# First slots of a fused attention and feed-forward kernel: one copy moved ahead of the exponentials, the weight pieces spread one to a slot, and one layout kept for the first chunk alone

## The chip, the cores and the metric

The kernel runs on one core of a Trainium2 chip. Times are microseconds of the device for one execution. Before the change the median of three runs is 655.12 us, from 654.51 to 655.52. The trace and the page of the profile come from a further execution, which took 657.56 us.

## The reference

Attention over a band, followed by two matrix products with a leaky ReLU between them:

```python
# q, k, v: (4 batches, 8 heads, 768 positions, 64)
scores = q @ k.T / 8 + bias            # bias: -slope[head] * distance
keep   = (key < n_global) | ((0 <= rel) & (rel < n_local))     # 8 and 96
a      = softmax(where(keep, scores, -1e9));   o = a @ v
x      = o.transpose(0, 2, 1, 3).reshape(3072, 512)
h      = x @ w_in                      # 512 x 2048, weights given as float64
out    = maximum(0.01 * h, h) @ w_out  # 2048 x 512
```

## The kernel before

**Attention units.** The attention is cut into 48 units `u` of one block of 128 queries and 4 heads, two units to a block, six blocks to a batch. Each unit has 192 gathered keys (128 in the first block of a batch). Here unit u passes through these steps:

- `scores(u)` (L181), TensorE: 8 small products, query and key, into PSUM.
- `biased(u)` (L195), VectorE: four instructions that add the bias and take the maximum.
- `exps(u)` (L210), ScalarE: four exponentials with their sums.
- `sums(u)` (L230, L231) on VectorE, then `dg` (L245) on GpSimd: reciprocals of the sums, put on diagonals.
- `transposes(u)` (L274), TensorE: 24 small products that transpose the probabilities and scale them by `dg`. Units from 14 on go another way, through DMAs.
- `keep_pt(u)` (L289, L293), ScalarE: the copy `pt` of the transposed probabilities out of PSUM. There is one buffer.
- `attn_v(u)` (L314, L326), TensorE: probabilities by values; called AV(u) below.
- `high_x(u)` (L339) on ScalarE and `low_x(u)` (L343) on VectorE: the result as two float32r parts, `xh` and `xl`.

`event(t)` puts these in a pipeline: AV(t-2), scores(t), transposes(t-1), then the work of the other engines, with `keep_pt(t-1)` last. So the copy of unit t-1 stands on ScalarE behind the exponentials of unit t, and AV(t-1) on TensorE in the next event waits for that copy.

**The `tall` layout.** For units 2 to 11 `tall(u)` is true: two of the three groups of keys lie on all 128 partitions, and AV uses 8 products of 128x64 (L326, `lhs, rhs = v[:, n, f, :], pt[:, n, f]`). Where it is false, the same keys lie on halves of 64 partitions, and there are 16 products of 64x64. `layout` on the host arranges `v` accordingly.

**FFN slots.** `order` is a list of pairs of a chunk (384 tokens, three blocks) and one of 16 column tiles of `w_in`. Slot j runs `ffn1(j)` (12 products, L797 to L799), then `ffn2(j-1)` (9 products, L818 to L820). The result of ffn1 is copied out by ScalarE (`t`, L801), goes through VectorE (L802), and becomes `gh` (ScalarE, L807) and `gl` (VectorE, L808). Events 0 to 7 run in a lead before the first slot; events 8 to 13 run in slots 1 to 6, one each, ahead of ffn1 in their slot.

**Weight pieces.** The float64 weights come in 32 pieces: piece 2f is column tile f of `w_in`, piece 2f+1 belongs to `w_out`. `conversion(p)` starts the loads of later pieces and returns three steps: `scale` (ScalarE, L560), `shift` (VectorE, L563 and L565) and `low` (VectorE, L569). Two more come after: `high` (ScalarE, L573) and `rest` (VectorE, L576). `conv_at` says which pieces a slot converts: the first of them goes with the event, others follow ffn1's steps. Up to the change piece 7 is converted before slot 0, and pieces 8 to 14 in slots 0 to 6. A piece's raw buffer is one of four (`STAGES`), freed by `low`.

**Order.** While `pinned[0]` holds, as it does here, each engine runs its instructions in the order in which the code issues them. The waits between engines are put in by the framework.

## Time and profile before

| | |
|---|---|
| median of three runs | 655.12 us (654.51 to 655.52) |
| profiled execution | 657.56 us, its span 656.0 us |
| TensorE matmuls | 632.2 us busy, 96% of the span |
| VectorE, ScalarE, GpSimd | 374.4, 283.0, 21.9 us busy |
| TensorE's granted clock | 0.99 over the span |

The page gives the busy time of each engine and the chain of work that ended last. The windows give busy time and granted clock of a stretch. A row of the timeline has start, duration, engine, line, operation, `out<-in`, shapes and a count; brackets at its end tell the idle time before it and what ended that. A float32 matmul of the small kind stands in the trace as two records, so that 8 products read x16.

### The profile page before, as it was taken

Reading aid. Unit: us, or ns where it says so; the run is one execution under the profiler, and the core shown is the slowest. Engines: PE = TensorE matmul, PEld = TensorE weight load, DVE = VectorE, ACT = ScalarE, POOL = GpSimd, SP = SyncE. Lnnn points to the kernel's source line nnn. Section 1 sums busy time; section 2 is a strip of 40 time slices with the busy share of each in tenths; the row PEclk is TensorE's granted clock in tenths of the full one; section 3 lists DMA queues with packets and bytes.
Section 4 is the critical chain, followed back from the end, with each engine's and each line's share of the span. In section 5 each row is a group of like instructions: output and inputs, shape, how many; then the busy total and the mean of one; then the engine's idle time right before and its main releaser. Section 6 shows DMA issues by size and latency. Waiting matters only on the chain.

```text
span 656.0 us, 14356 instructions
## 1 busy us (share of the span) xinstructions
PE 632.2 (96%) x5644; PEld 558.4 (85%) x5644; DVE 374.4 (57%) x1121; ACT 283.0 (43%) x796; POOL 21.9 (3%) x48
## 2 busy tenths in 40 slices
PE   5679999999999999999999999999999999999996
PEld 4568898988888888988989889889889889999985
DVE  6987778897667454654644645635645546232222
ACT  6976664555444342452443432443433524232221
POOL 3202210000000000000000000000000000000000
PEclk9898999999999999999999999999999999999998
DMA  8984444432766433443444444335343432010001
GB/s 278 348 305 148 163 164 144 139 97 95 217 208 224 137 85 113 142 153 112 162 129 138 148 129 122 126 106 175 121 137 131 153 118 90 8 49 1 0 1 52
DMA packets 55162, 88.04 MB, mean 134 GB/s; under 512 B 9776, under 2 KB 30256, under 8 KB 55088
## 3 DMA queue, kind: packets, MB, share of 16 engines
q1 hardware_dynamic: 55088, 87.06, 40.6%
q8 instruction: 46, 0.75, 0.5%
q14 instruction: 28, 0.23, 0.1%
HBM read 67.90 MB, written 19.14 MB: 133 GB/s over the span
## 4 chain that ended last, share of the span: by engine, by line
PE 89%; DVE 6%; ACT 2%; issue 1%; POOL 1%; DMA 0%; ACTq 0%; POOLq 0%; DVEq 0%
PE ps_h L797 14%; PE ps_o L820 13%; PE ps_h L798 13%; PE ps_h L799 13%; PE ps_o L818 13%; PE ps_o L819 13%; PE ps_v L181 2%; PE ps_v L326 2%; PE ps_av L181 1%; PE ps_v L314 1%; DVE w L569 1%; PE ps_av L326 1%; DVE w L565 1%; PE ps_tr L274 1%; PE ps_av L314 1%
## 5 line engine op out<-in xcount | busy, mean ns | idle before, releaser
L797 PE MATMUL ps_h<-xh,wih 128*128 128x384 f32 x512 | 175.8, 343 | 0.1
L798 PE MATMUL ps_h<-xl,wih 128*128 128x384 f32 x512 | 172.5, 337 | 0.0
L799 PE MATMUL ps_h<-xh,wil 128*128 128x384 f32 x512 | 172.3, 337 | 0.0
L802 DVE SCALAR_TENSOR_TENSOR t<-t 128x384 f32<-128x384 f32 x128 | 73.1, 571 | 144.7 <-ACT t L801 142.7
L801 ACT COPY t<-ps_h 128x384 f32<-128x384 f32 x128 | 61.3, 479 | 214.5 <-PE ps_h L799 214.5
L820 PE MATMUL ps_o<-woh,gl 128*128 128x512 f32 x384 | 152.1, 396 | 0.1
L818 PE MATMUL ps_o<-woh,gh 128*128 128x512 f32 x384 | 151.2, 394 | 1.0 <-ACT part L468 0.7
L819 PE MATMUL ps_o<-wol,gh 128*128 128x512 f32 x384 | 151.3, 394 | 0.0
L797 PEld LDWEIGHTS ps_h<-xh,wih 128*128 128x128 f32 x512 | 96.3, 188 | 10.3 <-ACT xh L339 3.1
L808 DVE TENSOR_TENSOR gl<-t,gh 128x384 fp32r<-128x384 f32 x128 | 71.3, 557 | 55.5 <-ACT gh L807 55.5
L798 PEld LDWEIGHTS ps_h<-xl,wih 128*128 128x128 f32 x512 | 96.3, 188 | 4.2
L799 PEld LDWEIGHTS ps_h<-xh,wil 128*128 128x128 f32 x512 | 96.2, 188 | 0.0
L807 ACT CAST gh<-t 128x384 fp32r<-128x384 f32 x128 | 65.5, 512 | 59.5 <-DVE t L802 58.7
L820 PEld LDWEIGHTS ps_o<-woh,gl 128*128 128x128 f32 x384 | 72.3, 188 | 18.0 <-DVE gl L808 2.2
L210 ACT ACTIVATE pr<-pr,nmall 128x192 f32<-128x192 f32 (+1 forms) x192 | 83.5, 438 | 3.6 <-DVE nmall L195 3.0
L818 PEld LDWEIGHTS ps_o<-woh,gh 128*128 128x128 f32 x384 | 72.2, 188 | 13.0 <-ACT part L468 1.2
L819 PEld LDWEIGHTS ps_o<-wol,gh 128*128 128x128 f32 x384 | 72.2, 188 | 11.2
L195 DVE CUSTOM_DVE_ANT_0 pr<-ps_v,nbw 128x192 f32<-128x192 f32 x88 | 25.3, 354 | 26.4 <-ACT xh L339 26.4
L210 ACT ACTIVATION_READ_ACCUMULATOR pr<-pr,nmall 128x1 f32 x192 | 36.4, 190 | 0.0
L237 DVE TENSOR_SCALAR pr<-pr,rs 128x192 f32<-128x192 f32 (+1 forms) x136 | 33.8, 312 | 1.0
L240 DVE STREAM_TRANSPOSE pr<-pr 128x768 f32<-128x768 f32 (+1 forms) x34 | 32.1, 945 | 0.9
L339 ACT CAST xh<-ps_v 128x256 fp32r<-128x256 f32 x28 | 10.5, 373 | 37.9 <-PE ps_v L181 36.2
(94 smaller groups left out, 462.7 us busy)
## 6 DMA issues: line engine op xcount, KB each, us to landing
kr<-in_kp_dram SPq DMA_DIRECT2D x40, 384.0 KB, 4.4
vr<-in_vp_dram SPq DMA_DIRECT2D x40, 320.0 KB, 4.5
via<-pr SPq DMA_DIRECT2D x30, 384.0 KB, 2.5
pt<-via SPq DMA_DIRECT2D x120, 96.0 KB, 2.3
wst<-in_wi_dram SPq DMA_DIRECT2D x16, 512.0 KB, 4.5
wst<-in_wo_dram SPq DMA_DIRECT2D x16, 512.0 KB, 3.9
qs<-in_qp_dram SPq DMA_DIRECT2D x24, 256.0 KB, 3.2
out_dram<-part SPq DMA_DIRECT2D x21, 256.0 KB, 2.1
```

Of the source, the lines that this page charges most:

```text
L210: pin(nc.scalar.activation(out=p, in_=p, func=AF.Exp, scale=-1.0, bias=nm[:, 2 * a + j:2 * a + j + 1], accum_out=sm[:, 2 * a + j:2 * a + j ...
L237: pin(nc.vector.tensor_scalar(out=p, in0=p, scalar1=rs[:, n:n + 1], scalar2=1.0, op0=ALU.mult, op1=ALU.mult))
L797: tc.keep_in_program_order(nc.tensor.matmul(ps, lhsT=wih[:, k, fs], rhs=xh[:, k, :CT], start=(k == 0), stop=False))
L798: tc.keep_in_program_order(nc.tensor.matmul(ps, lhsT=wih[:, k, fs], rhs=xl[:, k, :CT], start=False, stop=False))
L799: tc.keep_in_program_order(nc.tensor.matmul(ps, lhsT=wil[:, k, fs], rhs=xh[:, k, :CT], start=False, stop=(k == NK - 1)))
L801: pin(copy(out=t, in_=ps))
L802: pin(nc.vector.scalar_tensor_tensor(out=t, in0=t, scalar=0.01, in1=t, op0=ALU.mult, op1=ALU.max))
L807: pin(copy(out=gh, in_=t))
L808: pin(nc.vector.tensor_tensor(out=gl, in0=t, in1=gh.bitcast(F32), op=ALU.subtract))
L818: tc.keep_in_program_order(nc.tensor.matmul(o, lhsT=gh[:, ts_], rhs=woh[:, f, :], start=first, stop=False))
L819: tc.keep_in_program_order(nc.tensor.matmul(o, lhsT=gh[:, ts_], rhs=wol[:, f, :], start=False, stop=False))
L820: tc.keep_in_program_order(nc.tensor.matmul(o, lhsT=gl[:, ts_], rhs=woh[:, f, :], start=False, stop=last))
```

## The change

Four edits. `tall` holds for units 2 to 5 alone (`LEAD` is 6), and `layout` follows it. In events from 8 on `keep_pt(t-1)` is issued before `exps(t)`. Piece 7 is converted in slot 0, not ahead of the slots, and pieces 8 to 14 follow: slot 3 takes two, 10 and 11. The loop that ran the last parts of piece 6 and the whole of piece 7 ahead of slot 0 is gone; the parts of piece 6 now run among the steps of ffn1 in slot 0.

```diff
     def tall(u):
-        return u < BY_DVE and where(u)[2] > 0
+        return u < LEAD and where(u)[2] > 0
...
             if t == LEAD + 1:
                 high_x(t - 2, ov)
+            if mid and t >= LEAD + 2:
+                keep_pt(t - 1)
             exps(t)
...
         low()
-        if mid:
-            keep_pt(t - 1)
         if old and t <= LEAD:
             high_x(t - 2, ov)
+        if mid and t < LEAD + 2:
+            keep_pt(t - 1)
...
-    conv_at = {n: [n + LEAD_CONV + 1] for n in range(half)}
+    conv_at = {0: [7], 1: [8], 2: [9], 3: [10, 11], 4: [12], 5: [13], 6: [14]}
...
-    for step in (*due, *conversion(LEAD_CONV)):
-        if step in due:
-            due.remove(step)
-        step()
     behind = []
...
-    pe = [s for s in range(BY_DVE // NU) if s % NB]
+    pe = [s for s in range(CHUNKS[0]) if s % NB]
     vp[pe, :, :, :4] = vt[pe]
```

The lines below show instructions in the order in which an engine runs them. ScalarE, slots 0 and 1, before; the names `w_697`, `w_733`, `w_764`, `w_825` are pieces 6, 7, 8 and 9:

```order
L573 CAST wih<-w_697 128x4x128
L560 ACTIVATE w_733<-wst 128x512
L801 COPY t<-ps_h 128x384
L573 CAST woh<-w_733 128x512
L807 CAST gh<-t 128x384
L560 ACTIVATE w_764<-wst 128x512
L339 CAST xh<-ps_av 128x2x128
L573 CAST wih<-w_764 128x4x128
L560 ACTIVATE w_825<-wst 128x512
L210 ACTIVATE pr,sm<-pr,nmall 128x192 x4
L289 COPY pt<-ps_tr 128x2x6x64
```

The same stretch after, where lines below the edits have moved by two (L799 is L801 before) and `w_755`, `w_824` are pieces 7 and 8:

```order
L799 COPY t<-ps_h 128x384
L571 CAST wih<-w_697 128x4x128
L805 CAST gh<-t 128x384
L558 ACTIVATE w_755<-wst 128x512
L339 CAST xh<-ps_av 128x2x128
L571 CAST woh<-w_755 128x512
L558 ACTIVATE w_824<-wst 128x512
L289 COPY pt<-ps_tr 128x2x6x64
L210 ACTIVATE pr,sm<-pr,nmall 128x192 x4
```

Between the copy of slot 0's result and the copy `pt` of unit 7 there are now two scalings of weights (pieces 7 and 8) and two casts (6 and 7) and no exponentials; before, the cast of piece 6 and the scaling of piece 7 stood ahead of `t`, and the casts of 7 and 8, the scalings of 8 and 9 and the four exponentials behind it.

VectorE at the end of slot 3 and the start of event 11 before, where `w_1045` is piece 11:

```order
L802 SCALAR_TENSOR_TENSOR t<-t 128x384
L576 TENSOR_TENSOR wol<-w_1045,woh 128x512
L808 TENSOR_TENSOR gl<-t,gh 128x384
L195 ISA pr,nmall<-ps_av,nbw 128x192
L195 ISA nmall 128x1
```

The same place after, where `w_1060` is piece 10 and `w_1109` piece 11:

```order
L574 TENSOR_TENSOR wil<-w_1060,wih 128x4x128
L806 TENSOR_TENSOR gl<-t,gh 128x384
L561 TENSOR_SCALAR w_1109<-w_1109 128x512
L563 SCALAR_TENSOR_TENSOR w_1109<-wst,w_1109 128x512
L567 SCALAR_TENSOR_TENSOR w_1109<-wst,w_1109 128x512
L195 ISA pr,nmall<-ps_av,nbw 128x192
```

Three instructions for piece 11 stand between `gl` of slot 3 and `biased` of event 11; before, `gl` was followed by `biased` there.

TensorE at the start of slot 1 before (AV, scores, transposes, the first product of ffn1):

```order
L314 MATMUL ps_av<-pt,vr 64x128 x4
L326 MATMUL ps_av<-pt,vr 64x64 x8
L181 MATMUL ps_av<-kr,qs 64x192 x8
L274 MATMUL ps_tr<-dg,pr 64x64 x24
L797 MATMUL ps_h<-xh,wih 128x384
```

And after:

```order
L314 MATMUL ps_av<-pt,vr 64x128 x4
L326 MATMUL ps_av<-pt,vr 64x64 x16
L181 MATMUL ps_av<-kr,qs 64x192 x8
L274 MATMUL ps_tr<-dg,pr 64x64 x24
L795 MATMUL ps_h<-xh,wih 128x384
```

The second row goes from x8 to x16, here and in slots 2 to 6; the sizes in these rows are those of the result, so that the 128 or 64 partitions of the operands do not show. TensorE's order is otherwise the same, and so is GpSimd's. On SyncE's queue the loads of weight pieces 11 to 13 come one event later among the loads of queries, keys and values, and that of piece 14 comes behind the values of unit 11.

## The prediction

> **What bounds the kernel now.** I read the page first, then the waits of TensorE from the lead's end on, then the stretches around the one long wait.

> ```profile
> span 656.0 us, 14356 instructions
> PE 632.2 (96%) x5644; PEld 558.4 (85%) x5644; DVE 374.4 (57%) x1121; ACT 283.0 (43%) x796; POOL 21.9 (3%) x48
> ...
> PE ps_av L314 <- ACT pt L289: 3.5, 1, 3.5
> PE ps_o L818 <- ACT part L468: 0.7, 1, 0.7
> ```

> TensorE is the bound: 632 of 656 us. The last two rows are all that the list of its waits shows from 36 us to the end. So a saving counts where TensorE works or waits, and the one wait of size is that of AV(7) in slot 2 for the copy `pt` of unit 7.

> The windows (length, busy times, granted clock, DMA) show slot 1, the wait, slot 2, slot 3 and the rest:

> ```profile
> 38.82:45.96 7.14, 7.14 (x110) 5.83 (x109) 6.10 (x12) 3.58 (x8) 0.64 (x1) 1.00 0.70 234
> 45.96:49.50 3.54, 0.00 (x0) 0.00 (x1) 3.47 (x15) 3.54 (x12) 0.08 (x1) 0.87 0.91 323
> 49.50:59.00 9.50, 9.50 (x110) 7.99 (x110) 7.17 (x21) 6.35 (x17) 1.68 (x2) 0.69 0.48 165
> 59.00:65.90 6.90, 6.90 (x111) 5.90 (x110) 4.68 (x17) 4.47 (x14) 2.42 (x5) 1.00 0.45 124
> 84.00:650.00 566.00, 564.91 (x4433) 503.17 (x4432) 307.36 (x879) 220.75 (x607) 0.88 (x1) 1.00 0.37 117
> ```

> The wait costs twice. TensorE is idle for 3.54 us, with ScalarE busy for all of it. Then slot 2 takes 9.50 us where slot 3, with the same work, takes 6.90: the clock granted after the idle time is 0.69 over the slot. That is 2.60 us more, 6.14 together. After 84 us TensorE is idle for 1.09 us of 566.

> **Part 1: the copy and the pieces.** ScalarE and VectorE ahead of that wait, with SyncE's loads out of the picture:

> ```profile
> 38.33 0.66 DVE L569 SCALAR_TENSOR_TENSOR w<-wst,w 128x512 int32<-128x512 int32 x1
> 38.55 0.34 PE L799 MATMUL ps_h<-xh,wil 128*128 128x384 f32 x1
> 40.14 0.46 ACT L801 COPY t<-ps_h 128x384 f32<-128x384 f32 x1
> 43.92 0.42 DVE L563 TENSOR_SCALAR w<-w 128x512 int32<-128x512 int32 x1
> 45.11 0.69 DVE L569 SCALAR_TENSOR_TENSOR w<-wst,w 128x512 int32<-128x512 int32 x1
> 45.83 0.62 ACT L573 CAST wih<-w 128x512 fp32r<-128x512 f32 x1 [1.76 <-DVE w L569]
> 46.36 0.66 ACT L560 ACTIVATE w<-wst 128x512 f32<-128x512 f32 x1
> 46.92 0.44 ACT L210 ACTIVATE pr<-pr,nmall 128x192 f32<-128x192 f32 x1
> 48.67 0.78 ACT L289 COPY pt<-ps_tr 128x768 f32<-128x768 f32 x1
> 49.35 0.47 ACT L801 COPY t<-ps_h 128x384 f32<-128x384 f32 x1
> 48.87 0.17 DVE L230 TENSOR_SCALAR rs<-sm 128x4 f32<-128x4 f32 x1
> 49.42 0.88 POOL L245 TENSOR_TENSOR dg<-eye,rs 128x256 f32<-128x256 f32 x1 [9.96 <-DVE rs L231]
> 57.04 0.48 ACT L801 COPY t<-ps_h 128x384 f32<-128x384 f32 x1 [0.79 <-PE ps_h L799]
> 58.14 0.52 ACT L807 CAST gh<-t 128x384 fp32r<-128x384 f32 x1
> ```

> The result of ffn1(0) is there at 38.55 + 0.34 = 38.89, but its copy starts at 40.14, behind piece 7. The cast of piece 8 waits 1.76 us for `low` on VectorE, and `pt` comes behind that, a scaling, and 1.75 us of exponentials (46.92 to 48.67). The same durations in the new order give:

> - `t` of slot 0 at 38.95; `gh` 1.10 behind it (57.04 to 58.14), at 40.05, ending 40.57. The leftover parts of piece 6 fit beside: its `low` ends at 38.99.
> - `scale` of piece 7 from 40.47 to 41.15; `shift` and `low` take 1.88 (43.92 to 45.80), to 43.1. Its cast starts then; `scale` of piece 8 is 0.53 later (45.83 to 46.36), `pt` of unit 7 another 0.56 later (46.36 to 46.92), at 44.2, ending 44.97.
> - The exponentials of unit 8 start 0.68 behind it (48.67 to 49.35), at 44.9. Their sums come 1.95 later (46.92 to 48.87), `dg` starts 0.55 after that and lasts 0.88: it ends at 48.25.

> TensorE without a wait reaches AV(7) at 45.96 less the saving of part 2, 45.65. So `pt` is 0.7 us early and the wait goes, with the low clock behind it: 6.14 us.

> What is late next are the transposes, now behind `pt` and the exponentials. AV(7) and scores(9) take 0.73 + 0.70 us (rows of part 2), so transposes(8) are up at 47.08, and `dg` lets them go at 48.30: a new wait of 1.2 us in slot 2. I bound it by 0 and 2.07 (lead, below) and take 1.2. From there on slots recover: from `pt` to the next `pt` the ring is 0.68 + 1.95 + 0.55 + 0.88 and some 0.95 of transposes, 5.0 us, against a slot of 6.6.

> Slot 3 takes two pieces. The same walk, with 5.16 us from L274 to the next AV (60.74 to 65.90, rows of part 2): AV(8) at 48.30 + 5.16 = 53.46, scores(10) done at 53.46 + 0.73 + 0.88 = 55.07, then on ScalarE `xh` (about 0.3), `scale` (0.56) and `pt` (0.68): exps(10) at 56.7, their sums at 58.6, `low` of piece 10 to about 59.6. Behind it on VectorE come the leaky ReLU of slot 3 (0.6), with `gh` on ScalarE to 60.7, and `gl` to 61.2. Then VectorE spends 1.88 us on piece 11 ahead of `biased` of event 11 and of ScalarE's cast, to 63.1; 0.53 + 0.56 later, at 64.2, `pt` of unit 10 starts, exps(11) 0.68 later at 64.9, and `dg` ends 1.95 + 0.55 + 0.88 later, at 68.3. TensorE, by slots of 6.6, is at AV(10) at 66.64 (its `pt` is in time); with the shorter scores of unit 12 transposes(11) are up 1.2 us later, at 67.85: a wait of 0.5, bounds 0 and 1.3; I take 0.6, since each step of the walk can only be late. In the other slots the walk has `dg` 0.9 us or more ahead.

> Does a TensorE wait of 1.2 us lower the clock? The lead has both answers:

> ```profile
> 17.35 1.21 PE L274 MATMUL ps_tr<-dg,pr 64*64 64x64 f32 x48 [2.07 <-POOL dg L245]
> 25.48 0.57 PE L274 MATMUL ps_tr<-dg,pr 64*64 64x64 f32 x23 [1.44 <-POOL dg L245]
> 16.00:20.00 4.00, 2.65 (x80) 2.40 (x80) 3.93 (x16) 3.34 (x12) 0.88 (x1) 0.73 1.02 397
> 24.00:28.00 4.00, 2.27 (x84) 1.85 (x84) 3.93 (x16) 3.85 (x13) 0.88 (x1) 1.00 0.94 326
> ```

> A gap of 2.07 us goes with a clock of 0.73, one of 1.44 leaves it at 1.00. I take no loss at 1.2. [...]

> The rest has one answer each. SyncE: a load in the queue of piece 11 now waits for `low` of piece 7 (43.1) with the values of unit 9 behind it, which AV(9) needs at 60.0; the scaling of piece 11 comes at 60.6. Every piece is still complete a slot or more before its product (8 in slot 1 for slot 4, 11 in slot 4 for slot 6). If a load were late, TensorE would wait for the 4.5 us of its landing at most:

> ```profile
> wst<-in_wi_dram SPq DMA_DIRECT2D x16, 512.0 KB, 4.5
> 64.48 0.88 POOL L245 TENSOR_TENSOR dg<-eye,rs 128x256 f32<-128x256 f32 x1 [1.01 <-DVE rs L231]
> ```

> GpSimd stands idle for 1.01 us ahead of that `dg` although it rescales a table there; exponentials that come later only widen this.

> **Part 2: AV on halves.** AV in both layouts at full clock, the tall one of slots 3 and 4 and the other of later units:

> ```profile
> 59.00 0.45 PE L314 MATMUL ps_av<-pt,vr 64*64 64x128 f32 x8
> 59.38 0.73 PE L326 MATMUL ps_av<-pt,vr 128*64 128x64 f32 x16
> 60.04 0.88 PE L181 MATMUL ps_av<-kr,qs 64*64 64x192 f32 x16
> 60.74 0.88 PE L274 MATMUL ps_tr<-dg,pr 64*64 64x64 f32 x48
> 65.90 0.45 PE L314 MATMUL ps_av<-pt,vr 64*64 64x128 f32 x8
> ...
> 181.23 0.45 PE L314 MATMUL ps_av<-pt,vr 64*64 64x128 f32 x8
> 181.50 0.64 PE L326 MATMUL ps_av<-pt,vr 64*64 64x64 f32 x32
> 181.96 0.83 PE L181 MATMUL ps_av<-kr,qs 64*64 64x192 f32 x16
> ```

> From the first product of AV to the scores it is 60.04 - 59.00 = 1.04 us with 8 tall products, and 181.96 - 181.23 = 0.73 with 16 on halves: twice the records, 0.31 us less. Both ends shrink (0.38 to 0.27 ahead of L326, 0.66 to 0.46 behind), as if going over to the 128*64 form and back cost time each. Six units, 6 to 11: 1.86 us less, all on TensorE's path. Bounds: 0 and 2.0.

> **The sum.** 6.14 + 1.86 = 8.0 us saved, 1.2 + 0.6 of new waits, 6.2 net. The profiled execution would go from 657.56 to 651.4 (span 649.8); it stands 2.44 above the median of the runs, so from that, 655.12 - 6.2 = 648.9.

> **Rivals.**
> - *No new waits* (0.13): `dg` comes in time in slots 2 and 5. For it speaks the ring of 5.0 us, against it the walk. 655.12 - 8.0 = 647.1.
> - *The clock falls at the new wait* (0.07): the wait of slot 2 reaches 2 us, or the gate acts earlier than in the lead, and slot 2 loses its 2.6 us again. 651.5.
> - *ScalarE and VectorE are 2 us later in slot 1* (0.05), through the second scaling or a weight load. AV(7) then waits 1.3, `dg` is 3.2 late in all, the clock falls: 8.0 - 3.2 - 0.6 - 2.6 = 1.6 saved, 653.5.
> - *The records on halves cost what the tall ones do* (0.03): 0.66 / 16 = 41 ns each, 16 more are 0.66 us per unit, 4.0 in place of -1.9. Longer AVs hide 1.6 of the new waits, leaving 1.9 saved: 653.2. Against it stands the row of 32 records in 0.46 us, 14 ns each. [...]
> - *Slower* (0.03): the order `pt`, exponentials, sums, `dg`, transposes becomes the bound of the slots, with gaps at L274 over 2.07 us that drop the clock. One costs 2.07 + 2.6 = 4.7, two cost 9.4 against 8.0 saved: 656.5. It decides once the ring takes 6.6 + 2.07 = 8.7 us in two slots, 3.7 more than its rows add up to.
> - *It doesn't do what it says* (0.02): AV(7) still waits for `pt`, as something else stands ahead of it on ScalarE; only part 2 is left, and with new waits not even that. 655.

> **How the numbers follow.** The forecast, both new waits about as sized, has 0.67, from 648.0 to 650.2. A measurement here can tell about 0.2%, 1.3 us. The range takes in no new waits below (647.0) and the fallen clock above (651.5). Faster: 0.67 + 0.13 + 0.07 + 0.05 + 0.03, less a margin for what I have not seen: 0.93. Slower 0.03, within 0.2% 0.04.

> **What would show it.** The row of AV's wait for `pt` is gone from TensorE's waits, and the clock is 1.00 from 36 us on. In its place stand L274 waits for `dg`, once about 1.2 us near 47 and once about 0.6 near 68. AV in slots 1 to 6 reads x32 in the 64*64 form, with 0.73 us from L314 to L181. Slots 3 and 4 take 6.6 us. The prediction is wrong if a clock under 1.00 shows after 36 us, if waits at L274 recur in each slot, or if slots 1 to 6 together give back less than 5 us while TensorE has no wait there (the time then went to the lead or after 84 us).

## The result, and the profile after

The median of four runs each went from 655.32 to 651.36 us (ratio 0.9933, 95% interval 0.9908 to 0.9958), 4.0 us less. On two further occasions, beside the kernel before on the same chip, the ratios were 0.9915 (0.9896 to 0.9935) and 0.9929 (0.9905 to 0.9952): 5.6 and 4.7 us. 648.9 was forecast, in a range from 647.0 to 651.5.

The page after, and TensorE's waits from 36 us on. Lines below the edits have moved: L816 was L818, L795 was L797, L799 was L801.

```profile
span 650.7 us, 14540 instructions
PE 628.9 (97%) x5740; PEld 556.5 (86%) x5740; DVE 375.4 (58%) x1121; ACT 282.8 (43%) x796; POOL 22.2 (3%) x48
...
PE ps_av L326 <- issue: 1.3, 1, 1.3
PE ps_tr L274 <- POOL dg L245: 0.9, 1, 0.9
PE ps_o L816 <- ACT part L471: 0.7, 1, 0.7
PE ps_o L816 <- ACT gh L805: 0.2, 1, 0.2
```

AV's wait of 3.5 us for `pt` is gone. In its place stand a gap of 1.3 us that the profile puts down to no other engine ("issue"), and a wait of 0.9 for `dg`.

TensorE, ScalarE, VectorE and GpSimd around those places, from the timeline (start, duration):

```profile
38.43 0.45 PE L314 MATMUL ps_av<-pt,vr 64*64 64x128 f32 x8
40.27 0.52 PE L326 MATMUL ps_av<-pt,vr 64*64 64x64 f32 x21 [1.28 <-issue]
43.77 0.79 ACT L289 COPY pt<-ps_tr 128x768 f32<-128x768 f32 x1
44.45 0.46 ACT L210 ACTIVATE pr<-pr,nmall 128x192 f32<-128x192 f32 x1
46.43 0.17 DVE L230 TENSOR_SCALAR rs<-sm 128x4 f32<-128x4 f32 x1 [0.67 <-ACT pr L210]
46.98 0.88 POOL L245 TENSOR_TENSOR dg<-eye,rs 128x256 f32<-128x256 f32 x1 [7.89 <-DVE rs L231]
...
46.48 0.45 PE L314 MATMUL ps_av<-pt,vr 64*64 64x128 f32 x8
46.74 0.64 PE L326 MATMUL ps_av<-pt,vr 64*64 64x64 f32 x32
47.21 0.83 PE L181 MATMUL ps_av<-kr,qs 64*64 64x192 f32 x16
47.92 0.93 PE L274 MATMUL ps_tr<-dg,pr 64*64 64x64 f32 x48
...
68.44 0.93 PE L274 MATMUL ps_tr<-dg,pr 64*64 64x64 f32 x48 [0.88 <-POOL dg L245]
73.64 0.45 PE L314 MATMUL ps_av<-pt,vr 64*64 64x128 f32 x8
```

This execution is 0.39 us ahead at AV(6) (38.43 against 38.82). The walk of the prediction, less 0.39, had `pt` of unit 7 at 43.8, exps(8) at 44.5, the end of `dg` at 47.86, transposes(8) at 47.91 and AV(11) at 73.2. The rows have 43.77, 44.45, 46.98 + 0.88 = 47.86, 47.92 and 73.64. TensorE itself came to AV(7) at 46.48, where the walk less 0.39 had 45.26: the gap of 1.28 us at AV(6) lies between, and it takes up the time in which transposes(8) would have waited. AV on halves takes 47.21 - 46.48 = 0.73 us, as forecast.

The windows of slots 1, 2 and 5:

```profile
38.43:46.48 8.05, 6.77 (x127) 5.95 (x126) 6.82 (x20) 6.26 (x17) 0.66 (x1) 1.00 0.93 332
46.48:53.13 6.65, 6.65 (x127) 5.68 (x126) 6.25 (x21) 4.99 (x15) 1.24 (x2) 1.00 0.68 240
66.21:73.64 7.43, 6.55 (x126) 5.59 (x125) 6.52 (x22) 5.69 (x20) 2.72 (x6) 1.00 0.61 196
```

The clock is 1.00 in slot 2, where it was 0.69, and the slot takes 6.65 us where it took 9.50. From AV(6) to the start of ffn1 in slot 7 it is 79.64 - 38.43 = 41.21 us; before, 85.94 - 38.82 = 47.12. That is 5.9 us less in this pair, with 6.2 forecast from that profile. The open question was why medians show 4.0 to 5.6.

### The profile page after: what moved, and what is told of

The parts are those of the page before. It is cut to its first block, busy times and chain, and to the rows that moved or that the text cites. A ratio compares the mean times of both kernels' runs of the same rounds, so it can differ in the third digit from the quotient of the medians.

```text
span 650.7 us, 14540 instructions
## 1 busy us (share of the span) xinstructions
PE 628.9 (97%) x5740; PEld 556.5 (86%) x5740; DVE 375.4 (58%) x1121; ACT 282.8 (43%) x796; POOL 22.2 (3%) x48
## 4 chain that ended last, share of the span: by engine, by line
PE 89%; DVE 4%; ACT 3%; DMA 1%; issue 1%; POOL 0%; SPq 0%; POOLq 0%; DVEq 0%; ACTq 0%
PE ps_h L795 14%; PE ps_h L797 13%; PE ps_h L796 13%; PE ps_o L818 13%; PE ps_o L817 13%; PE ps_o L816 13%; PE ps_v L181 3%; PE ps_v L326 2%; PE ps_v L314 1%; DMA kr<-in_kp_dram 1%; PE ps_av L181 1%; ACT pr L210 1%; DVE w L567 1%; PE ps_av L326 1%; DVE w L563 1%
## 5 line engine op out<-in xcount | busy, mean ns | idle before, releaser
L795 PE MATMUL ps_h<-xh,wih 128*128 128x384 f32 x512 | 175.6, 343 | 0.1
L797 PE MATMUL ps_h<-xh,wil 128*128 128x384 f32 x512 | 172.4, 337 | 0.0
L799 ACT COPY t<-ps_h 128x384 f32<-128x384 f32 x128 | 61.2, 478 | 214.8 <-PE ps_h L797 214.8
L816 PE MATMUL ps_o<-woh,gh 128*128 128x512 f32 x384 | 151.2, 394 | 1.0 <-ACT part L471 0.7
L818 PE MATMUL ps_o<-woh,gl 128*128 128x512 f32 x384 | 152.0, 396 | 0.1
L795 PEld LDWEIGHTS ps_h<-xh,wih 128*128 128x128 f32 x512 | 96.0, 188 | 10.4 <-ACT xh L339 3.1
L797 PEld LDWEIGHTS ps_h<-xh,wil 128*128 128x128 f32 x512 | 96.0, 188 | 0.0
L805 ACT CAST gh<-t 128x384 fp32r<-128x384 f32 x128 | 65.7, 513 | 59.4 <-DVE t L800 58.6
L818 PEld LDWEIGHTS ps_o<-woh,gl 128*128 128x128 f32 x384 | 72.3, 188 | 17.8 <-DVE gl L806 2.0
L210 ACT ACTIVATE pr<-pr,nmall 128x192 f32<-128x192 f32 (+1 forms) x192 | 83.7, 441 | 3.5 <-DVE nmall L195 3.0
L816 PEld LDWEIGHTS ps_o<-woh,gh 128*128 128x128 f32 x384 | 72.2, 188 | 13.1 <-ACT part L471 1.1
L210 ACT ACTIVATION_READ_ACCUMULATOR pr<-pr,nmall 128x1 f32 x192 | 36.8, 192 | 0.0
## 6 DMA issues: line engine op xcount, KB each, us to landing
wst<-in_wi_dram SPq DMA_DIRECT2D x16, 512.0 KB, 4.2
wst<-in_wo_dram SPq DMA_DIRECT2D x16, 512.0 KB, 4.0
```

Source lines behind the costliest of these rows:

```text
L210: pin(nc.scalar.activation(out=p, in_=p, func=AF.Exp, scale=-1.0, bias=nm[:, 2 * a + j:2 * a + j + 1], accum_out=sm[:, 2 * a + j:2 * a + j ...
L795: tc.keep_in_program_order(nc.tensor.matmul(ps, lhsT=wih[:, k, fs], rhs=xh[:, k, :CT], start=(k == 0), stop=False))
L797: tc.keep_in_program_order(nc.tensor.matmul(ps, lhsT=wil[:, k, fs], rhs=xh[:, k, :CT], start=False, stop=(k == NK - 1)))
L799: pin(copy(out=t, in_=ps))
L805: pin(copy(out=gh, in_=t))
L816: tc.keep_in_program_order(nc.tensor.matmul(o, lhsT=gh[:, ts_], rhs=woh[:, f, :], start=first, stop=False))
```

## The experiments

Two theories for the missing time. A: the low clock behind the wait was read from one long execution and is worth less in the median. B: the changed kernel gives time back, in the gap of 1.3 us and the wait of 0.9. Neither covers the spread of the rest. From the start of ffn1(7) to the end of the span the products are the same in every kernel here, yet that stretch took from 567.9 to 571.1 us in the fourteen profiles (570.1 in the prediction's, 571.1 in the first of the changed kernel), and the lead up to AV(6) took from 38.1 to 41.3.

The number compared below is therefore the distance from AV(6) to ffn1(7), which covers slots 1 to 6, from the timelines (differences of start times):

| kernel | us | slots 1 and 2 | slot 5 |
|---|---|---|---|
| before, two profiles | 47.12, 45.42 | 20.18, 18.42 | 6.75, 6.74 |
| changed, three profiles | 41.21, 41.21, 41.38 | 14.70, 14.71, 14.88 | 7.43, 7.42, 7.38 |
| order_only | 42.01 | 14.71 | 7.00 |
| halves_only | 41.88 | 16.48 | 6.32 |
| conv_only | 41.90 | 14.90 | 6.70 |
| keep_only | 46.78 | 19.79 | 6.74 |
| before_filled | 44.74 | 17.75 | 6.70 |
| late_pair | 41.14 | 14.71 | 6.35 |
| no_pair | 40.21 | 14.72 | 6.35 |
| slot0_free | 43.31 | 14.60 | 6.33 |
| copy_behind | 40.02 | 14.51 | 6.32 |

**before_again: the kernel before, unchanged.**

> The kernel before, unchanged, for what differs between its own executions. Theory A (the clock term was read from one long execution): the stretch from AV(7) to AV(8), 9.50 us in the execution that the prediction used, is shorter in most executions, since the low clock covers less of it; spans spread over 2 us or more, and the median lies about 2 us under that execution. Theory B (the changed kernel gives time back): slot 2 takes about 9.5 us here in each execution, spans lie within 1 us of each other, and the missing time must be looked for in the changed kernel (a gap of 1.3 us in slot 1, a wait of 0.9 us in slot 5).

656.7 against 656.27 us (ratio 1.0002, 0.9987 to 1.0017); single executions of the kernel before lie from 654.1 to 658.9 on that chip. Windows of its wait, slot 2 and slot 3:

```profile
48.31:51.26 2.95, 0.00 (x1) 0.01 (x1) 2.88 (x11) 2.95 (x11) 0.08 (x1) 1.00 0.86 309
51.26:59.70 8.44, 8.44 (x109) 7.34 (x109) 7.17 (x21) 6.34 (x17) 1.68 (x2) 0.80 0.54 185
59.70:66.66 6.96, 6.96 (x110) 5.94 (x110) 4.74 (x17) 4.53 (x14) 2.41 (x5) 1.00 0.47 164
```

Wait and low clock cost 2.95 + (8.44 - 6.96) = 4.4 us here, and 6.14 in the profile of the prediction. That is theory A's sign. The spread doesn't come from there alone, though: AV(6) starts at 41.28 here and at 38.82 there, and this execution was the longest of its twelve (658.38) with the cheaper wait.

**order_only: the order and the pieces, without the new layout.**

```diff
-        return u < LEAD and where(u)[2] > 0
+        return u < BY_DVE and where(u)[2] > 0
```

(beside the changed kernel; `layout` likewise)

> The copy ahead of the exponentials and the pieces one slot later, with the tall layout for units 2 to 11 as before. By the prediction's terms: 6.1 us less than before, less about 0.6 us of waiting for dg in slot 2 and none in slot 5 (tall AVs are longer, dg is in time): 5.5 us saved. Theory A: 2.5 to 4 us saved, as the clock term is worth less. Theory B: 4 to 5.5 us. In both the wait of AV(7) for pt is gone and the clock is 1.00 in slot 2.

Ratio 0.9924 (0.9902 to 0.9946), 5.0 us less. In its profile transposes(8) wait 0.69 us for `dg`, as sized (0.6):

```profile
48.84 0.93 PE L274 MATMUL ps_tr<-dg,pr 64*64 64x64 f32 x48 [0.69 <-POOL dg L245]
```

5.0 is above what I wrote for theory A and within B's figures. With the 0.69 added back, wait and clock together are worth some 5.7 us here, which speaks against theory A's smaller clock term, though the interval (3.5 to 6.4 saved) holds less too.

**halves_only: the layout alone, beside the kernel before.**

```diff
-        return u < BY_DVE and where(u)[2] > 0
+        return u < LEAD and where(u)[2] > 0
```

> Only the layout: units 6 to 11 on halves, order and pieces as before. The wait of AV(7) for pt stays and takes in what AV(6) saves; AV(7) to AV(11) save 0.31 us each and AV(7), at a low clock, up to 0.6: 1.3 to 1.9 us less than before by the prediction, in theory A and B alike. If the rows on halves cost more in these slots than in the later ones, no gain or a loss.

Ratio 0.9957 (0.9941 to 0.9973), 2.8 us less (1.8 to 3.9), more than the 1.3 to 1.9 expected. Its wait and slots 2 and 3 show why a single profile is a poor price for the clock:

```profile
46.72:50.04 3.32, 0.00 (x1) 0.00 (x1) 3.25 (x13) 3.32 (x12) 0.08 (x1) 1.00 0.91 322
50.04:56.59 6.55, 6.55 (x126) 5.79 (x126) 6.46 (x20) 5.86 (x16) 1.68 (x2) 1.00 0.60 201
56.59:63.13 6.54, 6.54 (x127) 5.78 (x126) 5.65 (x19) 4.98 (x15) 2.41 (x5) 1.00 0.61 212
```

TensorE is idle for 3.32 us and the clock stays at 1.00: the same kind of gap cost 2.60 us in one execution, 1.48 in another and nothing here. Five AVs at 0.31 are 1.55 us. Slots 3 and 4 shrink by more than that: 6.54 us each, where they took 6.90 and 6.91. The rest of the 2.8 may be the clock or the spread, and isn't settled.

**before_filled: needless products in the wait.**

```diff
             ov = av = ps_x.tile([P, 2, 512], F32, tag="ps_av", name="ps_av")
+            if t == LEAD + 3:
+                for _ in range(12):
+                    tc.keep_in_program_order(nc.tensor.matmul(av[:, 0, :CT], lhsT=wih[:, 0, :P], rhs=xt[0][0][:, 0, :CT],
+                                                              start=True, stop=True))
             attn_v(t - 2, ov)
```

> The kernel before with 12 needless products of 128x384 ahead of AV(7), in the PSUM columns that the scores of unit 9 overwrite: they work in the time in which TensorE waits for pt, 2.1 us of it, so that the idle gap is about 1.2 us and not 3.3. AV(7) starts when it did. Theory A (part of the old cost was the clock, and it varies): slot 2 runs at clock 1.00 in 6.9 us, and the median is lower by the clock term alone, 1 to 2 us. If the clock term is the 2.6 us of the first profile in each execution: 2.6 less. If the clock doesn't matter for the median: the same time.

Ratio 0.9977 (0.9962 to 0.9992), 1.5 us less, interval 0.5 to 2.5. Doing more work made the kernel faster:

```profile
47.86 2.32 PE L365 MATMUL ps_av<-xh,wih 128*128 128x384 f32 x12 [1.44 <-DVE xl L343]
50.11 0.45 PE L314 MATMUL ps_av<-pt,vr 64*64 64x128 f32 x8
50.11:57.01 6.90, 6.90 (x111) 5.90 (x110) 6.63 (x20) 5.81 (x17) 1.55 (x2) 1.00 0.56 196
```

AV(7) starts no earlier than in the kernel before (10.85 us after AV(6); 10.68 and 9.98 there), and slot 2 runs at full clock in 6.90 us. So by this run the clock term is worth about 1.5 us in the median, with 2.60 just outside the interval. This is theory A's number. Other runs leave room for more: with a wait of 3.2 us (3.54 and 2.95 in the two profiles of the kernel before), order_only's 5.7 leaves 2.5 for the clock.

**conv_only and keep_only: the two halves of the order, beside the kernel before.** conv_only takes the new `conv_at` and drops the loop ahead of slot 0; keep_only moves the copy:

```diff
+            if mid and t >= LEAD + 2:
+                keep_pt(t - 1)
             exps(t)
...
-        if mid:
-            keep_pt(t - 1)
+        if mid and t < LEAD + 2:
+            keep_pt(t - 1)
```

> The pieces one slot later, with the copy pt still behind the exponentials and the layout as before. By the walk pt of unit 7 comes 1.75 us later than with the copy ahead, at 46.0 to 46.7, so AV(7) waits about 0.8 us; dg of unit 8 is 0.7 earlier and transposes(8) do not wait. Nearly all of order_only's gain is here: 4 to 4.6 us less than before. Rival: the copy's move carries the gain, and this one saves less than 2 us.

> The copy ahead of the exponentials alone, pieces and layout as before. pt of unit 7 comes 1.75 us earlier, so AV(7) waits 1.7 us in place of 3.3, but the exponentials of unit 8 end 0.7 later than before while TensorE is ahead, and transposes(8) wait for dg about 1.5 us. The waits move: 0.2 us saved, and the clock term (0 to 2 us) if two shorter gaps leave the clock up. Rival: the copy carries the gain, 4 us saved.

conv_only: ratio 0.9937 (0.9915 to 0.9960), 4.1 us less, with a wait of AV(7) for `pt` of 0.98 us and none for `dg`. keep_only: 0.9985 (0.9971 to 0.9999), 1.0 us less. The pieces carry the gain. The row of conv_only, and those of keep_only:

```profile
47.52 0.45 PE L314 MATMUL ps_av<-pt,vr 64*64 64x128 f32 x8 [0.98 <-ACT pt L289]
...
48.39 0.45 PE L314 MATMUL ps_av<-pt,vr 64*64 64x128 f32 x8 [1.80 <-ACT pt L289]
51.69 1.56 PE L274 MATMUL ps_tr<-dg,pr 64*64 64x64 f32 x48 [1.27 <-POOL dg L245]
48.39:59.22 10.83, 9.56 (x110) 8.08 (x110) 8.93 (x26) 8.06 (x25) 1.76 (x2) 0.68 0.61 210
```

The copy halves the wait of AV(7) and puts what it gains into a wait for `dg`, as walked (1.7 and 1.5 expected). The clock is 0.68 over the slot. By the windows (0.76 from 48 to 52 us, 0.50 from 52 to 56) it fell at about 50.07 us, before the second gap began (50.42): behind a gap of 1.80 us here, where it stayed behind one of 3.32 in halves_only.

**late_pair, no_pair, slot0_free: where the second piece goes, beside the changed kernel.**

```diff
-    conv_at = {0: [7], 1: [8], 2: [9], 3: [10, 11], 4: [12], 5: [13], 6: [14]}
+    conv_at = {0: [7], 1: [8], 2: [9], 3: [10], 4: [11], 5: [12, 13], 6: [14]}     # late_pair
+    conv_at = {0: [7], 1: [8], 2: [9], 3: [10], 4: [11], 5: [12], 6: [13, 14]}     # no_pair
+    conv_at = {1: [7], 2: [8], 3: [9], 4: [10, 11], 5: [12, 13], 6: [14]}          # slot0_free
```

> The changed kernel with its pair of pieces in slot 5 (12 and 13) and not in slot 3, so that piece 11 no longer stands ahead of biased of event 11. The wait of transposes(11) for dg in slot 5, 0.88 us in the changed kernel's profile, goes; piece 13 now delays unit 13, whose transposes come only in slot 23. Prediction: 0.6 to 0.9 us less than the changed kernel, so about 4.7 us less than before where the changed kernel has 4.0. [...]

late_pair: ratio 0.9920 (0.9897 to 0.9944), among the changed kernel's three (0.9915 to 0.9933), and 41.14 us: the 0.6 to 0.9 us expected were not gained. The wait in slot 5 is gone (6.35 us), but it comes back in slot 7, where ffn1 needs the buffer that ScalarE empties too late, behind the exponentials that piece 13 delayed:

```profile
78.75 0.45 ACT L799 COPY t<-ps_h 128x384 f32<-128x384 f32 x1
79.25 0.44 PE L795 MATMUL ps_h<-xh,wih 128*128 128x384 f32 x1 [0.78 <-ACT t L799]
```

> The changed kernel with one piece in each of slots 0 to 5 (7 to 12) and the pair 13 and 14 in slot 6, whose second piece stands ahead of no event. The wait for dg in slot 5 goes (0.9 us) and, other than with the pair in slot 5, nothing stands between the result of slot 6 and its copy t, so it isn't given back: 0.9 us less than the changed kernel, AV(11) 34.3 us after AV(6), and ffn1(7) 0.9 us earlier against AV(6). Rival: another wait takes it (the copy t or gl in slot 7), and the stretch from AV(6) to ffn1(7) is 41.2 us as in the changed kernel.

no_pair: ratio 0.9905 (0.9883 to 0.9928) where the changed kernel beside it had 0.9929, and 40.21 us in place of 41.2 to 41.4: by the traces the 0.9 us expected are gained and kept; the intervals of the times overlap.

> The changed kernel with no piece in slot 0: 7, 8, 9 in slots 1 to 3, pairs in slots 4 and 5. dg of unit 8 is then ready more than 1 us before transposes(8). It tells what the gap of 1.2 us at AV(6) costs. If the gap only covers a wait for dg that would come anyway, and depends on the order of ScalarE, it goes and slots 1 and 2 are 1.2 us shorter. [...]

slot0_free: ratio 0.9944 (0.9923 to 0.9965), slower than the changed kernel by the traces (43.31 us against 41.38), while the intervals overlap. Slot 1 keeps its gap (1.28 us, 8 records into L326 as in the changed kernel) with another order on ScalarE, and no_pair, whose order up to slot 2 is the changed kernel's, has none: so ScalarE's order is not its cause. The pairs bring a wait of 0.85 for `dg` in slot 6 and one of 1.99 for `t` in slot 7, behind which the products of ffn1 follow each other at 0.32 us from 83.15 to 86.03, where they do so at 0.17 in no_pair's slot 2:

```profile
41.13 0.52 PE L326 MATMUL ps_av<-pt,vr 64*64 64x64 f32 x21 [1.28 <-issue]
75.49 0.69 PE L274 MATMUL ps_tr<-dg,pr 64*64 64x64 f32 x32 [0.85 <-POOL dg L245]
82.59 0.44 PE L795 MATMUL ps_h<-xh,wih 128*128 128x384 f32 x1 [1.99 <-ACT t L799]
```

What the gap costs in the changed kernel is told by no_pair, whose slot 1 has none and whose slot 2 then waits for `dg`:

```profile
45.74 0.45 PE L314 MATMUL ps_av<-pt,vr 64*64 64x128 f32 x8
48.69 0.93 PE L274 MATMUL ps_tr<-dg,pr 64*64 64x64 f32 x48 [1.39 <-POOL dg L245]
```

Slots 1 and 2 take 14.72 us there and 14.70 to 14.88 with the gap. The gap lies in time that TensorE would have spent waiting for `dg`: beside that wait, the gap costs 0.2 us at most. One or the other is paid in full: without both, slots 1 and 2 take 6.54 (no_pair) and 6.55 us (halves_only), 1.6 less.

**after_third and copy_behind: the changed kernel, and it with the copy behind the exponentials again.** after_third runs the changed kernel as it is; after_again, on another occasion, did so too.

```diff
-            if mid and t >= LEAD + 2:
-                keep_pt(t - 1)
             exps(t)
...
-        if mid and t < LEAD + 2:
+        if mid:
             keep_pt(t - 1)
```

> The changed kernel once more, beside many executions of the kernel before on one chip. Terms as measured so far (wait about 3.2 us, low clock behind it of 0 to 2.6 and in the median some 1.5, AVs 1.9, new waits 1.2 and 0.9): 4.0 to 5 us less than before, and slot 2 at clock 1.00 in its profile. By the prediction's own sum: 6.2 less. The gap of 1.3 us at AV(6) stands in its profile again, and no wait for dg in slot 2 beside it.

> The changed kernel beside the three variants below on one chip: 4.5 to 5.5 us less than before. In its profile AV(11) starts 35.2 us after AV(6), with a gap of about 1.2 us at AV(6) and a wait of 0.9 us for dg in slot 5, as in the two profiles of it so far.

Ratios 0.9915 and 0.9929, 5.6 and 4.7 us less, the first of them more than the 4.0 to 5.0 expected; both profiles show about the same distance, gap and wait as the first.

> The changed kernel with the copy pt behind the exponentials in each event, as before the change. By the rows pt of unit 7 comes 1.75 us later and AV(7) waits; the gap at AV(6) covers 1.2 us of it, so 0.3 to 0.6 us of wait are left in slot 2; dg of units 8 and 11 is 0.7 us earlier, so slot 5 waits 0.2 and not 0.9. About the time of the changed kernel, within 0.5 us: the copy's move is worth next to nothing beside the pieces. Rival: the copy carries the gain, and this kernel is 2 us or more slower than the changed one.

copy_behind: ratio 0.9894 (0.9874 to 0.9915), 648.64 us where the changed kernel beside it had 650.62. It has the lowest ratio of the study, which overlaps with no_pair's. The two were expected within 0.5 us of each other. Its only wait in slots 1 to 6:

```profile
47.15 0.45 PE L314 MATMUL ps_av<-pt,vr 64*64 64x128 f32 x8 [1.34 <-ACT pt L289]
```

No wait for `dg` comes in slot 5 (6.32 us). From AV(6) to ffn1(7) it is 40.02 us, 1.2 less than in the changed kernel: beside the pieces, the copy's move costs time. The two intervals of the ratios overlap; the traces carry this, 0.2 of it in slots 1 and 2 and 1.1 in slot 5.

## Why the prediction was right or wrong

**The wait and the pieces: right.** The copy of slot 0's result moved from 40.14 to 38.53, `pt` of unit 7 from 48.67 to 43.77, and AV(7) no longer waits. The walk's steps on ScalarE and GpSimd came out within 0.1 us up to slot 2; TensorE came 1.2 us late to AV(7), by the gap at AV(6), which no step of the walk had. But the prediction gave this to both edits together. conv_only shows that the pieces alone save 4.1 us, and keep_only that the copy alone only moves the wait.

**The clock behind the wait: the term that was mis-sized.** I set it at 2.60 us from the one profile. It measured 2.60, 1.48 and 0 in three profiles with gaps of 3.54, 2.95 and 3.32 us, and 1.5 (0.5 to 2.5) in the median of before_filled. The wait itself was 3.54 and 2.95 in the two profiles of the kernel before. The prediction did state that its execution stood 2.44 us above the median, and then took the whole saving off the median all the same. An execution's length alone does not tell how long its terms are, though: before_again's was longer, and its wait and clock cost 4.4. With 3.2 + 1.5 the sum is 4.7 in place of 6.14; the runs leave it between that and 5.7.

**The rule for a fall of the clock: too simple.** I took it from single gaps (2.07 falls, 1.44 stays). The traces show more. In the profile of the kernel before, the clock is 0.50 from 17.83 to 21.24 us and from 48.55 to 55.37, so for 3.41 us and for twice that, and 1.00 between the two and from there to 652; the second fall comes 30.7 us after the first, nine times 3.41. In the first profile of the changed kernel it is 0.50 from 18.24 to 21.65 and 1.00 from there to 649. In the windows of before_again, order_only, halves_only, late_pair and keep_only a low stretch between 16 and 60 us adds up to about 3.4, 6.8 or 10.2 us. The table therefore cuts a profile into stretches of 3.41 us, counted from one of its own falls; the falls lie at other times in each execution. What goes with a fall there is the share of TensorE's busy time in the stretch just ahead, and not the length of the gap:

| profile | gap, us | busy share in the stretches of 3.41 us with the gap | clock at 0.50 |
|---|---|---|---|
| before | 3.54 | 0.24 | 48.55 to 55.37 |
| before_again | 2.95 | 0.66, 0.47 | 52.86 to 56.27 |
| halves_only | 3.32 | 0.50, 0.52 | nowhere |
| keep_only | 1.80 | 0.49 | 50.07 to 56.89 |
| slot0_free | 1.99 | 0.42 | 82.9 to 86.3 |
| before_filled | 1.44 | 0.58 | nowhere |
| no_pair | 1.39 | 0.59 | nowhere |

In these rows the clock fell behind shares of 0.24 to 0.49 and stayed behind 0.50 to 0.66. In the lead it fell behind 0.39 (the kernel before at 17.83, the changed one at 18.24), 0.45 (before_again at 32.4) and 0.50 (halves_only at 31.4): at 0.50 the traces show both. (For before, the stretch in which the clock was low already is left out. The times of before_again and keep_only are worked out from their windows, those of slot0_free from the products at 0.32 us. In before_filled and no_pair, which have no fall here to count from, the share is the least that one gap of that length leaves in 3.41 us; the clock is 1.00 in before_filled's windows from 40 to 60 us, and no product of ffn1 in no_pair's slot 2 shows the pitch of 0.32 us. Ahead of 14.4 us the traces of the kernel before and of the changed one have no record of the clock, so that part of the lead tells nothing.) The 2.60 us go with a low stretch of 6.8 us and the 1.48 with one of 3.4; the gap of 3.32 us, with nothing lost, lies across two stretches, 1.69 in one and 1.63 in the other. These are seven gaps of one kernel and its variants; why the clock falls was not shown. In the changed kernel's profile it is 1.00 from 36 to 649 us, as forecast, and a rival with 0.07 did not come true.

**AV on halves: right, and somewhat too small.** AV takes 0.73 us in slots 2 to 6 of the changed kernel and 32 records take 0.46 to 0.47, as forecast. The slots shrank by more than the 0.31 us read at AV, though: compared where neither layout waits, by 0.35 to 0.43 us each, 2.25 in all for 1.86 forecast and a bound of 2.0. Where the rest comes from is open. The rival that priced the records higher is out.

**The new waits: there, longer, and one in another place.** Slot 2 was to wait 1.2 us for `dg`. In the changed kernel's profile a gap of 1.28 in slot 1 took that time; where it is missing (no_pair) the wait is there, 1.39. That the gap cost no more on top was luck, as the prediction did not have it. Slot 5 waits 0.88, with 0.6 forecast and bounds of 0 and 1.3. By the lengths of the slots the two cost 1.6 and 1.1 us, 2.7 in all, where 1.8 was forecast.

**The sum with what was measured.** By the lengths of slots 1 to 6, the wait and the low clock cost 6.4 us in the prediction's profile and 4.7 in before_again; with 2.25 for the layout and less 2.7 for the gap and the wait that makes 5.9 and 4.2 us saved. The medians gave 4.0, 5.6 and 4.7 on the three occasions. That the prediction's 6.2 comes so near to the 5.9 of the first pair is luck in part: the layout was 0.4 too small and the new waits 0.9, and the errors work against each other. That the median fell inside the range was luck too: 651.36 lies 0.14 below an upper end that stood for a clock falling at the new wait, which did not happen. Why the first occasion came out lowest isn't shown; the spread outside slots 1 to 6 is large enough for it.

## What to carry to other kernels

Price a stall from several executions: what the clock lost behind one and the same wait was 2.60, 1.48 or 0 us, with gaps of 3.54, 2.95 and 3.32 us. When an engine's order holds up a stage, look for what is ahead of the late instruction that needn't be there (here the weight pieces); swapping two instructions, both of which the stage needs, only moves the wait from one consumer to the other. And spread the displaced work so that its last item lands ahead of nothing that the bounding engine waits for: a pair of pieces brought a wait of 0.9 us from slot 3, one of 0.8 from slot 5, and none from slot 6.
